# Banded attention and a mixture of adapters: wider q/k transposes, single PSUM banks, half-batch v slots and a planner that counts program fetches

## The chip, the cores and the metric

The kernel runs on one core of a Trainium2 chip. The metric is the device time of one execution in microseconds (us), lower is better. TensorE (PE in the profile) multiplies and transposes, VectorE (DVE), ScalarE (ACT) and GpSimd (POOL) do elementwise work, and SyncE (SP) issues transfers. All of them work from SBUF, the on-chip memory; TensorE writes its results to PSUM, a small memory of eight banks, from where VectorE and ScalarE carry them back to SBUF.

## The reference

q, k and v have 8 batches, 8 heads, 576 positions and 64 values per head, in 32-bit floats. Attention sees only 32 positions to each side. Its result, with the heads side by side, is a table of 4608 rows of 512, and goes through a mixture of 8 low-rank adapters of rank 16, of which each row uses the best two.

```python
scores = scale * np.matmul(q, k.transpose(0, 1, 3, 2))
mask = np.abs(pos[:, None] - pos[None, :]) <= window          # window = 32
attn = softmax(np.where(mask, scores, -1e9))
x = np.matmul(attn, v)  ->  [B * S, H * D] = [4608, 512]

logits = x @ w_gate                                           # [4608, 8]
w = softmax over the best two of the 8 logits
out = x + sum over these two experts e of  w * ((x @ A[e]) @ B[e])
```

## The kernel before

Work is in 16-bit floats. The heads of a batch are handled in pairs (4 pairs a batch, 32 in all), and one head of a pair lies in the upper 64 partitions, the other in the lower.

**Loads.** q and k are cut across batches into 9 tiles of 128 groups of 16 positions. GpSimd issues their loads (`load`), which also turn them to 16 bits. v comes on SyncE in four transfers a batch (`load_v`), and GpSimd casts each half batch with one instruction (`cast_v`) into a table with a column of ones, which later yields the softmax sum.

**Transposes.** `trans` turns a tile of q or k so that head values lie on partitions. It does so with 64x64 pieces: for each of 16 positions, both halves of the rows and both heads, which is 64 matmuls for a tile of q and 64 for one of k, each with its weight load. All go to one PSUM slot of two banks, and `evac` carries the slot out in one instruction, q on VectorE into `qT`, k on ScalarE into `kT`. The first tile is split into two halves.

**Attention.** `score` puts the mask into PSUM by four matmuls and adds 16 score matmuls; `expo` takes the exponential on ScalarE. There are 36 such groups. `pv` multiplies with v in 36 matmuls for a pair, and `norm` divides on VectorE and writes `xs`.

**Adapters.** Once a batch: `moe_xT` transposes x (20 matmuls), `moe_ex` carries that out on VectorE, `moe_zl` computes the low-rank product and the logits, `copy_z` brings these to SBUF, `gate1`, `gate_e` and `gate2` find the best two and their weights, `gate3` multiplies by the weights, `moe_zT` and `moe_ez` transpose, `moe_pd` multiplies with B and adds x, `moe_eo` carries out and `moe_st` stores in three parts. `gate3` runs on GpSimd, except in the last batch, where it runs on VectorE (`DIRECT`).

**Order.** No loop runs on the chip. Every piece of work is a task with an engine, an estimated duration, a due time, what it depends on, and the slots it takes and drops. `Planner.run` plays these tasks through in Python when the kernel is built: whenever an engine is free it starts the ready task with the earliest due time for which slots are left. The resulting order is written out as one straight program for each engine, and each engine then works in that order, waiting on semaphores for its inputs. So GpSimd, SyncE and the others stand before a waiting instruction with everything behind it waiting too. An estimate in the planner never delays anything on the chip by itself; it only moves tasks in that order.

**Slots.** PSUM is one pool `W` of four slots of two banks. v has two slots of a whole batch before the cast (`NVR`) and three after it (`NVB`), and the output five (`NOB`). `GATE` makes the load of k of tile t follow the cast of the first half of v of batch t - 2 in GpSimd's order, for t from 2 to 8; tile 1 has no such rule. `WDEP` names the v load after which the adapter weights are loaded.

Of the kernel before, what the change touches and what calls it, by code (L numbers as in the profile page):

```python
# [23 lines left out]
class Planner:  # L24
# [4 lines left out]
    STICK = 0.3  # L29
    SWITCH = 0.12  # L30

# [7 lines left out]

    def add(self, name, eng, dur, due, emit, deps=(), take=(), drop=(), lat=None, pkt=1.0,  # L40
            cap=1.0, mode=None):
        t = dict(name=name, eng=eng, dur=dur, due=due, emit=emit, deps=list(deps),
                 take=list(take), drop=list(drop), lat=self.LAT if lat is None else lat,
                 n=len(self.tasks), pkt=pkt, cap=cap, mode=mode)
        assert name not in self.by_name, name
        self.tasks.append(t)
        self.by_name[name] = t
        return name

    def run(self):  # L50
# [9 lines left out]
        held = {}  # L60
# [3 lines left out]
        done = []  # L64

# [21 lines left out]
        while events:  # L87
# [17 lines left out]
            while drops and drops[0][0] <= now + 1e-9:  # L105
                _, _, (p, key) = heapq.heappop(drops)
                self.slots[p].append(held.pop((p, key)))
            for e in engines:
# [3 lines left out]
                for t in sorted(ready[e], key=lambda t: (  # L112
                        t["due"] + (self.STICK if t["mode"] != last_mode else 0.0), t["n"])):
                    if all(self.slots[p] for p, _ in t["take"]):
                        break
                else:
                    continue
                ready[e].remove(t)
                for p, key in t["take"]:
                    s = self.slots[p].pop(0)  # L120
                    held[p, key] = s
                t["start"] = now
                end = now + t["dur"] + (self.SWITCH if t["mode"] != last_mode else 0.0)
                mode[e] = t["mode"]
# [21 lines left out]
def kernel(  # L146
# [35 lines left out]
    VQ = (("SP", 0.7, "Q1", nc.sync), ("SP", 0.7, "Q1", nc.sync))  # L182
    GATE = {t: [f"cv{t - 2}.0"] for t in range(2, 9)}
    GATE[1] = []
    WDEP = ["lv1.0.0"]
# [4 lines left out]
    NRAW, NKB, NVR, NVB, NPT, NX, NOB, NW = 3, 3, 2, 3, 6, 4, 5, 4  # L190
# [3 lines left out]
    vraw = [const.tile([128, NP * NB, D], F32, name=f"vraw{i}") for i in range(NVR)]  # L194
    vbd = [const.tile([128, NP * NB, VD], F16, name=f"vbd{i}") for i in range(NVB)]
# [9 lines left out]
    W16 = [w.bitcast(F16) for w in W]  # L205

# [10 lines left out]
    P.pool("W", NW)  # L217
# [8 lines left out]
    P.pool("rc", 3)  # L226
    place = {}

    def slot(p, key):
        return place[p, key]  # L230

# [50 lines left out]
    def vparts(b):  # L282
        return ((0, 18), (18, 36))

    def load_v(b, m0, m1, h):
        hh = (h + m0 // 18) % 2
        src = v[b].rearrange("(hh n) s d -> hh (n s) d", hh=2)[hh].rearrange(
            "(m p) d -> p m d", p=64)
        VQ[h][3].dma_start(out=vraw[slot("vr", b)][64 * h:64 * h + 64, m0:m1], in_=src[:, m0:m1])

# [30 lines left out]
    for b in range(B):  # L321
        for n, (m0, m1) in enumerate(vparts(b)):
            for h in range(2):
                due = 4 * b - 5.8 + 0.5 * n + 0.2 * h - (2 if b == B - 1 else 0)
                P.add(f"lv{b}.{n}.{h}", VQ[h][0], VQ[h][1], due,
                      lambda b=b, m0=m0, m1=m1, h=h: load_v(b, m0, m1, h),
                      prev, take=[] if n or h else [("vr", b)], lat=1.2)
                prev = [f"lv{b}.{n}.{h}"]
                P.add(f"dv{b}.{n}.{h}", VQ[h][2], 2.15 * (m1 - m0) / 36, 0, None, prev, lat=0.8,
                      pkt=14.7, cap=0.82)  # L330
    P.add("ldw", "SP", 2.0, -2, load_w, WDEP, lat=1.2)
    P.add("dw", "Q1", 1.7, -10, None, ["ldw"], lat=0.8, pkt=18.0)
# [3 lines left out]
    def cast_v(b, m0, m1):  # L336
        o = vbd[slot("vb", b)][:, m0:m1, 0:D]
        i_ = vraw[slot("vr", b)][:, m0:m1]
        nc.gpsimd.affine_select(out=o, in_=i_, compare_op=ALU.is_ge, fill=0.0,  # L339
                                base=1, channel_multiplier=0,  # L340
                                pattern=[[0, m1 - m0], [0, D]])

    for b in range(B):
        vp = vparts(b)
        for m, (m0, m1) in enumerate(vp):
            P.add(f"cv{b}.{m}", "POOL", 0.15 + 0.064 * (m1 - m0), 4 * b + 2 * m / len(vp) - 1.5,
                  lambda b=b, m0=m0, m1=m1: cast_v(b, m0, m1),
                  [f"dv{b}.{m}.{h}" for h in range(2)] + ([f"cvb{b}"] if b < NVB else [])
                  + ([f"cv{b}.{m - 1}"] if m else []),
                  take=[] if m else [("vb", b)], drop=[("vr", b)] if m == len(vp) - 1 else [])  # L350


    def trans(t, w, h0, h1):
        src = raw[2 * slot("raw" + "qk"[w], t) + w]
        tp = W16[slot("W", ("t", t, w, h0))].rearrange("p (h r i) -> p h r i", h=2, i=64)
        for r in range(RR):
            for h in range(h0, h1):
                p = slice(64 * h, 64 * h + 64)
                for hh in range(2):
                    nc.tensor.matmul(out=tp[64 * hh:64 * hh + 64, h, r],  # L360
# [3 lines left out]
    def evac(t, w, h0, h1):  # L364
        tp = W16[slot("W", ("t", t, w, h0))].rearrange("p (h r i) -> p h r i", h=2, i=64)[:, h0:h1]
        if w == 0:
            nc.vector.tensor_copy(  # L367
                out=qT[:, :, PADQ + 128 * t + 64 * h0:PADQ + 128 * t + 64 * h1].rearrange(
                    "p r (h i) -> p h r i", i=64),
                in_=tp)  # L370
        else:
            nc.scalar.copy(  # L372
                out=kT[slot("kT", t)][:, 64 * h0:64 * h1].rearrange("p (h i) r -> p h i r", i=64),
                in_=tp.rearrange("p h r i -> p h i r"))

    for t in range(NTI):
        hs = ((0, 1), (1, 2)) if t in SPLIT else ((0, 2),)
        for w in range(2):
            for y, (h0, h1) in enumerate(hs):
# [3 lines left out]
                P.add(f"tr{t}.{w}.{y}", "PE", 1.05 if f == 1 else 0.75,  # L383
# [3 lines left out]
                      take=[("W", ("t", t, w, h0))] + ([("kT", t)] if w and y == 0 else []),  # L387
                      drop=[("raw" + "qk"[w], t)] if last else [])
                P.add(f"e{'qk'[w]}{t}.{y}", "ACT" if w else "DVE",
                      (0.2 + 1.5 * f) if w else (0.12 + 1.1 * f), due,  # L390
                      lambda t=t, w=w, h0=h0, h1=h1: evac(t, w, h0, h1),
                      [f"tr{t}.{w}.{y}"], drop=[("W", ("t", t, w, h0))])
# [6 lines left out]
    def score(t):  # L399
        ps = W[slot("W", ("s", t))].rearrange("p (e i c) -> p e i c", e=2, c=128)  # L400
# [22 lines left out]
    def expo(t):  # L423
        nc.scalar.activation(out=PTs[slot("PT", t)].rearrange("p e i c -> p (e i c)"),  # L424
                             in_=W[slot("W", ("s", t))],
# [12 lines left out]
    for t in range(NT):  # L438
        need = set()
        for g in blocks(t):  # L440
            lo, hi = 4 * g - 2, 4 * g + 5
            for z in (max(lo, 0), min(hi, NI - 1)):
                tt = z // 128
                need.add((tt, (z % 128) // 64 if tt in SPLIT else 0))
# [3 lines left out]
              dep + ["mask", "pad", "ident"], take=[("W", ("s", t)), ("PT", t)], drop=drop)  # L448
# [4 lines left out]
    def pv(u):  # L453
        b, n = divmod(u, NP)
        e, m = divmod(n, 2)
        po = W[slot("W", ("p", u))].rearrange("p (h c) -> p h c", h=2)
        vb = vbd[slot("vb", b)]

        def one(hh, hb, j):
# [8 lines left out]
                rhs=vb[p0:p0 + 64, NB * n + a, :],  # L468
# [9 lines left out]
    def norm(u):  # L478
        b, n = divmod(u, NP)
        po = W[slot("W", ("p", u))].rearrange("p (h c) -> p h c", h=2)[:, :, 0:NG * VD]  # L480
# [13 lines left out]
    for k_, u in enumerate(order):  # L494
# [3 lines left out]
        if k_ % NP == NP - 1:  # L498
            drop.append(("vb", b))
# [4 lines left out]
              take=[("W", ("p", u)), ("rc", u)] + ([("xs", b)] if n == 0 else []), drop=drop)  # L504
# [5 lines left out]
    GX = ((0, 1, 2, 3), (4,))  # L510

    def moe_xT(b, j):
        x = xs[slot("xs", b)]
        tp = W16[slot("W", ("x", b, j))]
        for m, g in enumerate(GX[j]):
# [5 lines left out]
    def moe_ex(b, j):  # L521
        n = len(GX[j])
        nc.vector.tensor_copy(  # L523
            out=xT[b % 2][:, GX[j][0]:GX[j][0] + n].rearrange("p g c k -> p (g c k)"),
            in_=W16[slot("W", ("x", b, j))][:, 0:512 * n])

    def moe_zl(b):
        pz = W[slot("W", ("z", b))]
# [11 lines left out]
    def copy_z(b):  # L540
        pz = W[slot("W", ("z", b))][:, 0:GS * NG].rearrange("p (g c) -> p g c", c=GS)
        nc.scalar.copy(out=zls[b % 2], in_=pz[:, :, 0:ER + E])

    def zlog(b):
        if b in DIRECT:
            pz = W[slot("W", ("z", b))][:, 0:GS * NG].rearrange("p (g c) -> p g c", c=GS)
# [23 lines left out]
    def gate3(b):  # L570
        z = zlog(b)[0]
        lm, m2, s, gate = (gt[x][b % 2] for x in ("lm", "m2", "s", "gate"))
        eng = nc.vector if b in DIRECT else nc.gpsimd
# [3 lines left out]
    def moe_zT(b):  # L577
        zs = zss[b % 2].rearrange("p g e r -> p g (e r)")
        tp = W16[slot("W", ("y", b))]
# [4 lines left out]
    def moe_ez(b):  # L584
        tp = W16[slot("W", ("y", b))][:, 0:128 * NG]
# [3 lines left out]

    def moe_pd(b, j):  # L590
        pd = W[slot("W", ("d", b, j))].rearrange("p (i c) -> p i c", c=DD)
# [8 lines left out]
    def moe_eo(b, j):  # L600
        n = len(GG[j])
        pd = W[slot("W", ("d", b, j))].rearrange("p (i c) -> p i c", c=DD)
        nc.scalar.copy(out=obs[slot("ob", (b, j))][:, 0:n], in_=pd[:, 0:n])  # L603

    def moe_st(b, j):
        ob = obs[slot("ob", (b, j))]
        if len(GG[j]) == 2 and j:
            r0 = S * b + 128 * GG[j][0] - 32
            nc.sync.dma_start(out=out[r0:r0 + 256].rearrange("(i p) c -> p i c", p=128), in_=ob)
            return  # L610
        for i, g in enumerate(GG[j]):
            lo, hi = (32 if g == 0 else 0), (96 if g == NG - 1 else 128)
            r0 = S * b + 128 * g - 32
            nc.sync.dma_start(out=out[r0 + lo:r0 + hi], in_=ob[lo:hi, i])

    for b in range(B):
        d0 = 4 * b + 4.6
        for j in range(2):
            n = len(GX[j])
            P.add(f"xT{b}.{j}", "PE", 0.24 * n, d0 + 0.1 * j, lambda b=b, j=j: moe_xT(b, j),  # L620
                  [f"nm{u}" for u in range(4 * b, 4 * b + 4)]
                  + ([f"zl{b - 2}"] if b >= 2 else []), take=[("W", ("x", b, j))], mode="full")
            P.add(f"exx{b}.{j}", "DVE", 0.1 + 0.28 * n, d0 + 0.1 * j - 0.5, lambda b=b, j=j: moe_ex(b, j),
                  [f"xT{b}.{j}"], drop=[("W", ("x", b, j))])
        P.add(f"zl{b}", "PE", 1.29, d0 + 0.5, lambda b=b: moe_zl(b),
              [f"exx{b}.{j}" for j in range(2)] + ["cw"], take=[("W", ("z", b))], mode="full")
        dr = b in DIRECT
        if not dr:
            P.add(f"cz{b}", "ACT", 0.85, d0 - 1, lambda b=b: copy_z(b), [f"zl{b}"]
# [4 lines left out]
        P.add(f"g2{b}", "DVE", 1.15, d0 - 1, lambda b=b: gate2(b), [f"ge{b}"])  # L634
# [59 lines left out]
```

## Time and profile before

| what | before |
|---|---|
| time, median of 3 runs | 166.75 us (165.22 to 166.88) |
| span of the profiled execution | 167.0 us, mean TensorE clock 0.877 of full |
| all transfers | 29.34 MB, mean 176 GB/s |
| v loads | 32 of 288 KB, median 7.3 us from issue to landing |
| transposes of q and k (L360) | 1152 matmuls, busy 18.6 us |
| carrying them out (L367, L372) | VectorE 1222 ns a tile, ScalarE 1870 ns a tile |
| carrying out x (L523) | VectorE 1220 ns and 412 ns a batch |
| gate product (L574, L575) | GpSimd 253 and 1277 ns; VectorE, in the last batch, 201 and 825 ns |

The profile is one execution. Line numbers (L360) are those of the kernel before. Busy times of TensorE overlap, since its matmuls run in a pipeline, so the sum of a row says little about how long a group holds the engine; the time from one group's start to the next does. Each wait is put down to the event that ended it; "issue" stands where the profile shows no such event. The clock is the share of its full speed that TensorE was granted.

### The profile page before, as it was taken

Reading aid. Unit: us, or ns where it says so; the run is one execution under the profiler, and the core shown is the slowest. Engines: PE = TensorE matmul, PEld = TensorE weight load, DVE = VectorE, ACT = ScalarE, POOL = GpSimd, SP = SyncE. Lnnn points to the kernel's source line nnn. Section 1 sums busy time; section 2 is a strip of 40 time slices with the busy share of each in tenths; the row PEclk is TensorE's granted clock in tenths of the full one; section 3 lists DMA queues with packets and bytes.
Section 4 is the critical chain, followed back from the end, with each engine's and each line's share of the span. In section 5 each row is a group of like instructions: output and inputs, shape, how many; then the busy total and the mean of one; then the engine's idle time right before and its main releaser. Section 6 shows DMA issues by size and latency. Waiting matters only on the chain.

```text
span 167.0 us, 7557 instructions
## 1 busy us (share of the span) xinstructions
PE 104.2 (62%) x3464; PEld 77.2 (46%) x3464; DVE 67.8 (41%) x164; ACT 83.6 (50%) x94; POOL 54.0 (32%) x76
## 2 busy tenths in 40 slices
PE   0259536480975857736478678775667989386350
PEld 0247425470864634326457554544457467274110
DVE  0011520270745625225265834763460958542300
ACT  3214706432044497584036479744669796416160
POOL 7950710745030779800000683900063030210000
PEclk9999955558589999996789999999999999959785
DMA  5999999999979669999996279999630254404434
GB/s 86 215 222 224 189 215 226 212 203 206 214 180 205 116 122 183 215 253 221 342 231 164 50 103 253 296 183 216 225 98 4 92 205 145 142 4 147 138 112 171
DMA packets 49008, 29.34 MB, mean 176 GB/s; under 512 B 39632, under 2 KB 39632, under 8 KB 48976
## 3 DMA queue, kind: packets, MB, share of 16 engines
q1 hardware_dynamic: 43824, 19.42, 44.2%
q0 software_dynamic: 5152, 9.44, 33.3%
q8 instruction: 27, 0.44, 1.1%
q14 instruction: 5, 0.04, 0.1%
HBM read 28.85 MB, written 9.44 MB: 229 GB/s over the span
## 4 chain that ended last, share of the span: by engine, by line
PE 39%; issue 30%; DMA 12%; DVE 6%; ACT 4%; POOL 4%; POOLq 1%; ACTq 1%; SPq 0%; DVEq 0%
PE W L518 6%; PE W L465 5%; PE W L360 5%; DMA vraw<-in_v_dram 5%; PE W L594 5%; DMA raw<-in_q_dram 5%; PE W L416 5%; PE W L596 4%; PE W L531 4%; PE W L404 4%; POOL vbd L339 2%; DMA out_dram<-ob 2%; DVE xs L484 2%; ACT PT L424 2%; DVE qT L367 1%
## 5 line engine op out<-in xcount | busy, mean ns | idle before, releaser
L424 ACT ACTIVATE PT<-W 128x1024 f16<-128x1024 f32 x36 | 35.6, 1031 | 29.1 <-PE W L416 25.0
L360 PE MATMUL W<-ident,raw 64*64 64x64 f16 x1152 | 18.6, 210 | 21.4 <-issue 10.9
L465 PE MATMUL W<-vbd,PT 64*64 64x65 f16 x1152 | 19.0, 205 | 16.0 <-issue 11.5
L339 POOL TENSOR_SCALAR_AFFINE_SELECT vbd<-vraw 128x1152 f16<-128x1152 f32 x16 | 20.3, 1274 | 25.6 <-DMA vraw<-in_v_dram 25.5
L603 ACT COPY ob<-W 128x1024 f32<-128x1024 f32 (+1 forms) x24 | 20.6, 872 | 15.7 <-PE W L596 13.0
L360 PEld LDWEIGHTS <-raw 64*64 64x64 f16 x1152 | 16.3, 123 | 22.9 <-issue 12.8
L484 DVE TENSOR_TENSOR xs<-W,rc 128x640 f16<-128x640 f32 x32 | 26.4, 825 | 1.1
L372 ACT COPY kT<-W 128x2048 f16<-128x2048 f16 (+1 forms) x10 | 17.0, 1698 | 18.7 <-PE W L360 18.7
L465 PEld LDWEIGHTS <-PT 64*64 64x64 f16 x1152 | 15.4, 118 | 21.0 <-issue 17.2
L483 DVE RECIPROCAL rc<-W 128x10 f32<-128x10 f32 x32 | 6.9, 217 | 42.2 <-PE W L465 41.3
L416 PE MATMUL W<-qT,kT 64*64 64x128 f16 x576 | 20.4, 246 | 4.3 <-issue 2.8
L574 POOL TENSOR_TENSOR gate<-lm,s 128x40 f32<-128x40 f32 x7 | 1.8, 253 | 65.0 <-DVE s L568 65.0
L416 PEld LDWEIGHTS <-kT 64*64 64x64 f16 x576 | 17.0, 124 | 10.1 <-issue 7.3
L367 DVE COPY qT<-W 128x2048 f16<-128x2048 f16 (+1 forms) x10 | 11.2, 1116 | 24.0 <-PE W L360 24.0
L518 PE MATMUL W<-ident,xs 128*128 128x128 f16 x160 | 14.2, 253 | 6.5 <-issue 5.5
L404 PE MATMUL W<-mask,ident 64*64 64x512 f16 x144 | 17.9, 458 | 0.0
L523 DVE COPY xT<-W 128x2048 f16<-128x2048 f16 (+1 forms) x16 | 12.5, 816 | 10.9 <-PE W L518 10.9
L594 PE MATMUL W<-Bsb,zT 128*128 128x512 f16 x40 | 16.4, 409 | 0.8 <-ACT zT L586 0.8
L518 PEld LDWEIGHTS <-xs 128*128 128x128 f16 x160 | 12.3, 126 | 8.4 <-issue 6.0
L596 PE MATMUL W<-xs,po__107 128*128 128x512 f16 x40 | 16.0, 401 | 0.0
L531 PE MATMUL W<-WA,xT 128*128 128x136 f16 x160 | 11.4, 226 | 1.7 <-issue 1.2
L531 PEld LDWEIGHTS <-xT 128*128 128x128 f16 x160 | 10.0, 99 | 3.0 <-issue 1.3
(40 smaller groups left out, 82.3 us busy)
## 6 DMA issues: line engine op xcount, KB each, us to landing
vraw<-in_v_dram SPq DMA_DIRECT2D x32, 288.0 KB, 7.3
out_dram<-ob SPq DMA_DIRECT2D x8, 512.0 KB, 9.9
out_dram<-ob SPq DMA_DIRECT2D x16, 192.0 KB, 3.6
out_dram<-ob SPq DMA_DIRECT2D x8, 256.0 KB, 2.9
raw<-in_k_dram POOLq DMA_DIRECT2D x4, 256.0 KB, 6.8
raw<-in_q_dram POOLq DMA_DIRECT2D x4, 256.0 KB, 6.1
raw<-in_k_dram POOLq DMA_DIRECT2D x2, 448.0 KB, 6.5
raw<-in_q_dram POOLq DMA_DIRECT2D x2, 448.0 KB, 7.7
```

Of the source, the lines that this page charges most:

```text
L339: nc.gpsimd.affine_select(out=o, in_=i_, compare_op=ALU.is_ge, fill=0.0, base=1, channel_multiplier=0, pattern=[[0, m1 - m0], [0, D]])
L360: nc.tensor.matmul(out=tp[64 * hh:64 * hh + 64, h, r], lhsT=src[p, hh, D * r:D * r + D], rhs=ident[p, p], is_transpose=True, start=True, s ...
L404: nc.tensor.matmul(out=ps[o0:o0 + 64, e], lhsT=ident[p0:p0 + 64, p0:p0 + 64], rhs=bcast(mask[p0:p0 + 64].rearrange("p h r s -> p (h r s)") ...
L416: nc.tensor.matmul(out=ps[o0:o0 + 64, e, i], lhsT=kT[slot("kT", g // 32)][p0:p0 + 64, c1:c1 + 4].rearrange("p s r -> p (s r)"), rhs=qT[p0: ...
L424: nc.scalar.activation(out=PTs[slot("PT", t)].rearrange("p e i c -> p (e i c)"), in_=W[slot("W", ("s", t))], func=AF.Exp, scale=1.0 / floa ...
L465: nc.tensor.matmul(out=po[o0:o0 + 64, hh, c0:c0 + VD], lhsT=PTs[slot("PT", s // 4)][p0:p0 + 64, e, s % 4, 64 * (1 - j):64 * (1 - j) + 64], ...
L484: nc.vector.tensor_tensor(out=xs[slot("xs", b)].rearrange("p g (h m d) -> p h g m d", h=2, d=D)[:, :, :, n], in0=pog[:, :, :, 0:D], in1=bc ...
L518: nc.tensor.matmul(out=tp[:, o:o + 128], lhsT=x[:, g].rearrange("p (k c) -> p c k", c=4)[:, c], rhs=ident, is_transpose=True, start=True, ...
L531: nc.tensor.matmul(out=pz[:, GS * g:GS * g + ER + E], lhsT=xT[b % 2][:, g, c, :], rhs=WA_sb[:, c, :], start=(c == 0), stop=(c == NP - 1))
L594: nc.tensor.matmul(out=pd[:, i], lhsT=zTs[b % 2][:, g], rhs=B_sb, start=True, stop=False)
L596: nc.tensor.matmul(out=pd[:, i], lhsT=po_, rhs=x[:, g], start=False, stop=True)
L603: nc.scalar.copy(out=obs[slot("ob", (b, j))][:, 0:n], in_=pd[:, 0:n])
```

## The change

The edits, in the order of the code:

- The planner gets an estimate of program fetches: TensorE tasks say how many matmuls they hold (`ni`), and each crossing of 128 matmuls (`LINE`) costs at least 3.6 us since the last (`FETCH`). Due times get an offset for each kind of task (`LEAN`), and several duration estimates are altered.
- PSUM becomes one pool `H` of eight single banks. Work that needs two takes an even bank and the next (`"W"`), the rest takes one.
- Transposes of q and k of all tiles but the first use all 128 rows and 64 columns: 32 matmuls for each instead of 64. Each half of the result has a bank, and is carried out by an instruction of its own.
- x is transposed and carried out in parts of 2, 2 and 1 row groups, instead of 4 and 1.
- v slots hold half a batch: five before the cast and six after it. A pool `ring` of three limits, in the planner alone, how many v transfers are under way. The adapter weights come after all of v of batch 1.
- The load of k of tile 1 is to follow the first cast of v. The rule for the other tiles is the same as before.
- `gate3` runs on VectorE in every batch.
- The output has four slots instead of five.

```diff
+    LEAN = {"cv": 4.05, "cvb": 0.12, "cz": 1.73, "ek": 3.86, "eo": 4.52, "eq": 0.17,
...
+    LINE = 128
+    FETCH = 3.6
+
+    def fetched(self, t, now, end):
+        pos, n = self.pos, t["ni"]
+        self.pos = pos + n
+        k = -(-(pos + 1) // self.LINE) * self.LINE
+        late = 0.0
+        while n and k < pos + n:
+            at = now + late + (end - now) * (k - pos) / n
+            late += max(0.0, self.line - at)
+            self.line = max(at, self.line) + self.FETCH
+            k += self.LINE
+        return end + late
...
+                if e == "PE":
+                    end = self.fetched(t, now, end)
...
-    GATE = {t: [f"cv{t - 2}.0"] for t in range(2, 9)}
-    GATE[1] = []
-    WDEP = ["lv1.0.0"]
+    GATE = {t: [f"cv{t - 2}.0"] for t in range(2, NTI)}
+    GATE[1] = ["cv0.0"]
+    WDEP = ["lv1.1.1"]
...
-    NRAW, NKB, NVR, NVB, NPT, NX, NOB, NW = 3, 3, 2, 3, 6, 4, 5, 4
+    NRAW, NKB, NVR, NVB, NPT, NX, NOB, NW = 3, 3, 5, 6, 6, 4, 4, 4
+    HV = NP * NB // 2
...
-    vraw = [const.tile([128, NP * NB, D], F32, name=f"vraw{i}") for i in range(NVR)]
-    vbd = [const.tile([128, NP * NB, VD], F16, name=f"vbd{i}") for i in range(NVB)]
+    vraw = [const.tile([128, HV, D], F32, name=f"vraw{i}") for i in range(NVR)]
+    vbd = [const.tile([128, HV, VD], F16, name=f"vbd{i}") for i in range(NVB)]
...
-    P.pool("W", NW)
+    P.pool("H", 2 * NW)
...
+    def trans_full(t, w):
+        src = raw[2 * slot("raw" + "qk"[w], t) + w]
+        for r in range(RR):
+            tp = H16[slot("H", ("t", t, w, r // 8))]
+            for hh in range(2):
+                nc.tensor.matmul(out=tp[64 * hh:64 * hh + 64, 128 * (r % 8):128 * (r % 8) + 128],
+                                 lhsT=src[:, hh, D * r:D * r + D], rhs=ident,
+                                 is_transpose=True, start=True, stop=True)
...
+    def evac(t, w, h):
+        if t not in SPLIT:
+            tp = H16[slot("H", ("t", t, w, h))].rearrange("p (r i) -> p r i", i=128)
+            if w == 0:
+                c0 = PADQ + 128 * t
+                nc.vector.tensor_copy(out=qT[:, 8 * h:8 * h + 8, c0:c0 + 128], in_=tp)
+            else:
+                nc.scalar.copy(out=kT[slot("kT", t)][:, :, 8 * h:8 * h + 8],
+                               in_=tp.rearrange("p r i -> p i r"))
+            return
...
-    GX = ((0, 1, 2, 3), (4,))
+    PB = {1: "H", 2: "W"}
...
-        eng = nc.vector if b in DIRECT else nc.gpsimd
+        eng = nc.vector
```

## The prediction

> **What bounds the kernel now.** I read the queues and waits of the page first, then the waits of TensorE alone, its timeline, the table by stage, and last GpSimd's timeline.
>
> The page, parts 1 and 3 (busy time; DMA queue: packets, MB, share):
>
> ```profile
> PE 104.2 (62%) x3464; PEld 77.2 (46%) x3464; DVE 67.8 (41%) x164; ACT 83.6 (50%) x94; POOL 54.0 (32%) x76
> ...
> q8 instruction: 27, 0.44, 1.1%
> ```
>
> No engine is full. The second line is the clue: 27 packets carry instructions. 3464 matmuls and as many weight loads are 6928 instructions; 6928 / 27 = 257 to a packet, so one packet brings 128 matmuls with their weight loads. I call that a line of the program; there are 3464 / 128 = 27.1.
>
> The waits of TensorE (who waited <- releaser: us, times, longest):
>
> ```profile
> PE W L465 <- issue: 11.5, 7, 4.0
> PE W L360 <- issue: 10.9, 6, 2.6
> PE W L360 <- DMA raw<-in_k_dram: 6.8, 2, 5.8
> PE W L518 <- issue: 5.5, 3, 3.4
> PE W L581 <- DVE zs L575: 3.1, 1, 3.1
> ...
> PE W L416 <- issue: 2.8, 3, 1.2
> ...
> PE W L581 <- POOL zs L575: 2.3, 1, 2.3
> ...
> PE W L531 <- issue: 1.2, 1, 1.2
> ```
>
> "issue" is waiting that no semaphore explains: 11.5 + 10.9 + 5.5 + 2.8 + 1.2 = 31.9 us in 20 pieces, 1.6 us each. The DMA waits are nearly all the first one, before anything has landed. The timeline of TensorE shows what the pieces are:
>
> ```profile
> 37.27 0.44 PE L465 MATMUL W<-vbd,PT 64*64 64x65 f16 x25
> 41.69 0.38 PE L465 MATMUL W<-vbd,PT 64*64 64x65 f16 x11 [3.98 <-issue]
> ```
>
> TensorE stops in the middle of one group of 36 matmuls that needs nothing new. Counting matmuls along that timeline, the restarts at 62.69, 69.16, 75.36, 81.55, 86.38, 90.38, 95.20 and 98.93 us are exactly 128 matmuls apart, whatever stands there. So TensorE waits for its own program. Restart to restart takes 3.5 to 7.8 us, of which 0.5 to 4.0 us is the stop.
>
> The table by stage says why the trip is long (columns: window, width, busy us of each engine, granted clock, DMA share, GB/s):
>
> ```profile
> 20.00:48.00 28.00, 15.42 (x537) 12.68 (x538) 10.51 (x18) 9.35 (x9) 9.42 (x13) 0.57 1.06 202
> 48.00:92.00 44.00, 29.64 (x1080) 22.23 (x1080) 18.75 (x43) 24.02 (x28) 14.27 (x19) 0.92 0.94 208
> 92.00:120.00 28.00, 19.05 (x728) 13.86 (x729) 15.01 (x36) 18.08 (x21) 11.74 (x14) 1.00 0.84 181
> 120.00:145.00 25.00, 20.52 (x742) 14.76 (x737) 14.76 (x42) 18.28 (x22) 5.50 (x6) 1.00 0.39 131
> ```
>
> To 92 us the DMA engines are full with q, k and v[...]; from 116 us on, with few loads left, restarts are 3.5 to 5.1 us apart. From 20 to 145 us the bound is TensorE's program supply, on DMA engines that are nearly a bound themselves.
>
> GpSimd's timeline:
>
> ```profile
> 69.10 1.18 POOL L279 DMA_DIRECT2D raw<-in_q_dram  x2
> 93.18 0.25 POOL L574 TENSOR_TENSOR gate<-lm,s 128x40 f32<-128x40 f32 x1 [22.91 <-DVE s L568]
> 93.51 1.27 POOL L575 TENSOR_TENSOR zs<-zl,gate 128x640 f16<-128x640 f32 x1
> ```
>
> Its queue stands 22.9 us before a gate product, with the load issues of the next tile behind it.
>
> [...]
>
> **The change, part by part.**
>
> Transposes. For 8 of 9 tiles, q and k, 64 matmuls become 32: 8 x 2 x 32 = 512 fewer. 3464 - 512 = 2952, or 23.1 lines instead of 27.1: 4 trips less. Each new matmul moves 128 columns over all rows, on two halves of the columns. Nearest row: the score matmuls move 128 columns on four quarters, 16 of them in 0.24 us (at 90.96 us in the chain of waits), so 60 ns for the four at once; on two halves that is 30 ns each and 32 x 30 = 1.0 us. Ends: 0.85 us by the column rate alone (the 128x512 matmuls take 0.22 us, so 53 ns for 128 columns), and 2.0 us if the halves do not overlap. The 64 old ones take about 0.63 us (in the same chain 0.54 for 63 at 58.81 us, 0.70 for 64 at 65.97 us). I take 1.0: 16 x 0.37 = 6 us more TensorE work[...].
>
> What that does to stalls. From 20 to 145 us: 125 us less 32 of stall and about 5 of other waits leaves 88 us of work. The table has 537 + 1080 + 728 + 742 = 3087 matmuls there, 24.1 lines, so 3.7 us a line. After: 7 of the 8 tiles lie in the window, so 88 + 5 = 93 us and 3087 - 448 = 2639 matmuls, 20.6 lines, 4.5 us a line. Restart to restart periods in before were (us) 6.4, 4.5, 7.8, 6.5, 4.5, 6.5, 6.2, 6.2, 4.8, 4.0, 4.8, 3.7, 5.9, 4.8, 6.7, 3.5, 5.1, 3.7. Taken as trips, what is over 4.5 sums to about 17 us. So stall falls from 32 to about 17, work rises by 5: TensorE gains 10 us. Most of the extra transposing is free because it fills time that was stall.
>
> Gate product to VectorE. GpSimd loses 1.8 + 8.9 us; VectorE gains 7 x (0.20 + 0.825) = 7.2 us (its rows for the last batch). The engine handover goes, and GpSimd's queue no longer stops for it. On TensorE's path: the 2.3 us wait at L581, at 146 us, mostly goes. I count 2. The 3.1 us of the last batch stays; it was on VectorE already. Loads go out earlier, but TensorE hardly waits for raw after 20 us, so that by itself is worth nothing.
>
> Evacuations by halves. q on VectorE: 16 x 0.69 instead of 8 x 1.22, +1.3 us. xT: 2 x 0.69 instead of 1.22 a batch, +1.3 us. k on ScalarE: 16 x 1.01 instead of 15.0, +1.2 us. VectorE comes to 78 us, ScalarE to 85, in over 140: hidden beside TensorE. Halves come free sooner, but TensorE shows few waits for PSUM (2.3 for PT, 0.9 for xs), so single banks gain at most 1 us; counted 0.
>
> v by half batches. The same 32 loads of 288 KB. SyncE waited only 2.6 us for a v slot, TensorE 0.3 us for a cast. Counted 0, as are the smaller output ring (4 for 5; three stores a batch against a batch every 11 us or more) and the deeper memsets.
>
> The added wait: tile 1's k load now follows the first cast of v on GpSimd. It went out at 7.18, the cast was at 10.16, so k goes 4 us later and the q behind it 1.2 us later; TensorE's transposes of tile 1 (18.09 us) wait for them. Against that, v has less traffic beside it. Between -1.5 and +1.2 us; counted 0.
>
> Planner. Charging 3.6 us a line and shifted due times alter the order on every engine. No row prices this. Nothing lost if TensorE stays full, up to 8 us gained if stalls fall on idle spots; I count 3.
>
> Sum: 166.75 - 10 - 2 - 3 = 151.75, put at 151.
>
> **Rivals.** (a) The supply sets all of it: a line costs its trip whatever is in it. Then 4 lines x 4.9 us = 20 us and the 2 of the gate go: 145. For it: the exact 128 spacing. Against: 4.5 us of work a line nears the trip. (b) The DMA engines take the gain: loads come closer together, trips lengthen, each boundary still stalls 1.6 us. Then 4 x 1.6 = 6.4 saved, 5 spent on transposes, 2 for the gate: 163. For it: DMA at 0.94 to 92 us, and loads that cannot end much before 115. Against: 47 us remain after the last load, in which DMA is at a third. (c) Slower: the two halves do not overlap and each group takes 2.0 us. 16 x 1.4 = 22 us more, of which stalls hide 15, and the new order loses 0 to 4: 171 to 177, say 172. [...] Against: quarters overlap well today.
>
> **How the numbers follow.** The forecast 0.54, (a) 0.22, (b) 0.14, (c) 0.10. The forecast spreads from 147 to 157 with the planner's 0 to 8. The range 142 to 164 takes in the forecast, three quarters of (a) and half of (b): 0.54 + 0.16 + 0.07 = 0.77, near 8 in 10. Faster by over 1%: all but (c) and the slow end of (b), 0.87. Within 1%: 0.04. Slower: 0.09.
>
> **What would show it.** Right: 23 instruction packets; "issue" waits of TensorE at 13 to 21 us; a transpose group of 32 in 0.85 to 1.1 us; no gate product on GpSimd, and no idle stretch of 20 us between its load issues; the last 20 us, from the last transposes of x to the store, as before. Wrong: issue waits still near 32 us (b), under 10 with the same work (a), transposes at 2 us (c), or a new wait of TensorE for q, k or v of over 5 us after 20 us.

## The result, and the profile after

| | before | after |
|---|---|---|
| time, median | 165.99 us (163.64 to 166.88, 4 runs) | 156.05 us (155.06 to 157.51, 4 runs) |
| ratio, 95% interval | | 0.947 (0.931 to 0.963) |
| span of the profiled execution | 167.0 us | 153.4 us |

Faster by 5%, inside the range of 142 to 164, but 5 us short of the 151 that was forecast. Times of runs are medians, and each ratio comes from runs on the same chip as those of the kernel before, whose median was 165.8 to 168.4 us on the chips used. The ratios compare only the faster executions of each kernel, so they differ by up to 2% from the ratio of the medians beside them. Executions of one kernel scatter by 1 to 7% from the fastest to the slowest, so differences of a per cent between chips mean nothing.

The page after, parts 1 and 3:

```profile
PE 108.3 (71%) x2952; PEld 80.6 (53%) x2952; DVE 80.1 (52%) x197; ACT 84.1 (55%) x102; POOL 43.4 (28%) x62
...
q8 instruction: 23, 0.38, 1.0%
```

2952 matmuls in 23 packets: four trips fewer. The waits of TensorE after:

```profile
PE W L546 <- issue: 6.7, 6, 2.0
...
PE W L419 <- issue: 4.8, 2, 2.4
PE W L662 <- DVE zs L656: 3.2, 1, 3.2
PE W L419 <- DMA raw<-in_q_dram: 2.6, 1, 2.6
...
PE W L497 <- issue: 2.0, 3, 0.9
...
PE W L599 <- issue: 0.6, 1, 0.6
```

Waits without a releaser sum to 14.1 us, from 31.9; the forecast was about 17. The price is in the timeline of TensorE:

```profile
57.27 1.08 PE L419 MATMUL W<-ident,raw 128*64 128x128 f16 x32
58.29 0.39 PE L680 MATMUL W<-Bsb,zT 128*128 128x512 f16 x1
```

From the start of a group of 32 wide transposes to the start of what follows it is 1.02 us (forecast 1.0). The stages after:

```profile
20.00:48.00 28.00, 19.90 (x595) 16.31 (x591) 12.65 (x25) 12.98 (x14) 9.64 (x12) 0.94 1.12 214
48.00:92.00 44.00, 34.92 (x979) 26.43 (x982) 29.41 (x72) 28.56 (x37) 14.41 (x18) 0.96 0.97 207
92.00:120.00 28.00, 24.15 (x728) 17.35 (x716) 19.41 (x48) 20.25 (x26) 6.47 (x6) 1.00 0.85 205
```

Between 20 and 48 us TensorE is busy for 19.9 us where it was 15.4, and its waits without a releaser fall there from 10.8 to 4.4 us. The clocks printed for this stage, 0.94 and 0.57, cannot be set against each other: 32 wide transposes at 24.03 us took 1.92 us, nearly twice the 1.08 us of those at 28.85 us, although the clock printed for both is 1.00. GpSimd's timeline after has no gate product, but its queue does not run free:

```profile
84.16 1.19 POOL L346 DMA_DIRECT2D raw<-in_q_dram  x2
97.38 1.27 POOL L401 TENSOR_SCALAR_AFFINE_SELECT vbd<-vraw 128x1152 f16<-128x1152 f32 x1 [12.03 <-DMA vraw<-in_v_dram]
```

The idle stretch before the gate product is gone; one of 12 us, before a cast of v, stands between the load issues. TensorE's last wait for q or k ends at 24.03 us and it has none for a cast of v, so the 12 us do not reach it.

### The profile page after: what moved, and what is told of

The parts are those of the page before. It is cut to its first block, busy times and chain, and to the rows that moved or that the text cites. A ratio compares the mean times of both kernels' runs of the same rounds, so it can differ in the third digit from the quotient of the medians.

```text
span 153.4 us, 6568 instructions
## 1 busy us (share of the span) xinstructions
PE 108.3 (71%) x2952; PEld 80.6 (53%) x2952; DVE 80.1 (52%) x197; ACT 84.1 (55%) x102; POOL 43.4 (28%) x62
## 3 DMA queue, kind: packets, MB, share of 16 engines
HBM read 28.85 MB, written 9.44 MB: 250 GB/s over the span
## 5 line engine op out<-in xcount | busy, mean ns | idle before, releaser
L505 ACT ACTIVATE PT<-W 128x1024 f16<-128x1024 f32 x36 | 35.2, 1036 | 16.0 <-PE W L497 15.4
L565 DVE TENSOR_TENSOR xs<-W,rc 128x640 f16<-128x640 f32 x32 | 26.4, 824 | 1.1
L419 PE MATMUL W<-ident,raw 128*64 128x128 f16 x512 | 19.0, 232 | 8.9 <-issue 4.8
L546 PE MATMUL W<-vbd,PT 64*64 64x65 f16 x1152 | 17.5, 199 | 8.9 <-issue 6.7
L419 PEld LDWEIGHTS <-raw 128*64 128x64 f16 x512 | 16.6, 117 | 11.2 <-issue 10.4
L546 PEld LDWEIGHTS <-PT 64*64 64x64 f16 x1152 | 13.8, 111 | 14.5 <-issue 11.3
L444 ACT COPY kT<-W 128x1024 f16<-128x1024 f16 x16 | 15.7, 1021 | 9.3 <-PE W L419 9.2
L604 DVE COPY xT<-W 128x1024 f16<-128x1024 f16 (+1 forms) x24 | 13.6, 594 | 10.3 <-PE W L599 8.8
L442 DVE COPY qT<-W 128x1024 f16<-128x1024 f16 x16 | 10.6, 686 | 12.7 <-PE W L419 11.9
L564 DVE RECIPROCAL rc<-W 128x10 f32<-128x10 f32 x32 | 6.9, 215 | 15.3 <-PE W L546 13.8
L599 PE MATMUL W<-ident,xs 128*128 128x128 f16 x160 | 12.3, 229 | 1.5 <-DVE xT L604 0.8
L599 PEld LDWEIGHTS <-xs 128*128 128x128 f16 x160 | 10.4, 118 | 2.8 <-issue 1.7
L433 PE MATMUL W<-ident,raw 64*64 64x64 f16 x128 | 4.3, 239 | 9.2 <-POOL mask L318 6.0
```

Of the source, the lines that this page charges most:

```text
L419: nc.tensor.matmul(out=tp[64 * hh:64 * hh + 64, 128 * (r % 8):128 * (r % 8) + 128], lhsT=src[:, hh, D * r:D * r + D], rhs=ident, is_transp ...
L546: nc.tensor.matmul(out=po[o0:o0 + 64, hh, c0:c0 + VD], lhsT=PTs[slot("PT", s // 4)][p0:p0 + 64, e, s % 4, 64 * (1 - j):64 * (1 - j) + 64], ...
L565: nc.vector.tensor_tensor(out=xs[slot("xs", b)].rearrange("p g (h m d) -> p h g m d", h=2, d=D)[:, :, :, n], in0=pog[:, :, :, 0:D], in1=bc ...
L599: nc.tensor.matmul(out=tp[:, o:o + 128], lhsT=x[:, g].rearrange("p (k c) -> p c k", c=4)[:, c], rhs=ident, is_transpose=True, start=True, ...
```

## Experiments

**The changed kernel again, on a second chip.**

> The changed kernel once more, on the chip of these comparisons: 155 to 158 us, 0.93 to 0.96 of the kernel before.

156.64 us against 168.35, ratio 0.920 (0.912 to 0.928), a little below the expected 0.93 to 0.96. Issue waits are 16.1 us. So the change is worth 5 to 8%, depending on the chip's runs.

**Wide transposes alone, in the old order.**

```diff
 def trans(t, w, h0, h1):
...
+    if t not in SPLIT:
+        tw = W16[slot("W", ("t", t, w, h0))].rearrange("p (r i) -> p r i", i=128)
+        for r in range(RR):
+            for hh in range(2):
+                nc.tensor.matmul(out=tw[64 * hh:64 * hh + 64, r],
+                                 lhsT=src[:, hh, D * r:D * r + D], rhs=ident,
+                                 is_transpose=True, start=True, stop=True)
+        return
```

(`evac` reads the new layout, still with one instruction a tile; not shown.)

> The kernel before, in its own order and with its own slots; only the transposes of 8 tiles are 128x64, 32 matmuls for 64. Program supply theory: 23 instruction packets, TensorE's issue waits fall from 32 us to about 17, a transpose group rises from 0.63 to 1.0 us, time near 156 us (153 to 160). Order theory (the gain comes from the planner's new order): issue waits may fall, but other waits take their place, and the time stays at 163 to 167 us. DMA theory (the transfers are the bound): the same, 163 us or more.

160.4 us against 168.35 on the same chip as the run above, ratio 0.935 (0.929 to 0.942): 10 to 12 us by the ratio and 8 by the medians, from this one edit. The waits of TensorE:

```profile
PE W L480 <- issue: 7.6, 4, 3.1
...
PE W L533 <- issue: 3.0, 2, 2.5
PE W L546 <- issue: 2.8, 2, 2.4
PE W L596 <- POOL zs L590: 2.3, 1, 2.3
```

7.6 + 3.0 + 2.8 = 13.4 us of issue waits, 18.5 less than before. The order and the DMA theories fall for this part: nothing else of the change was in this kernel, the other waits of TensorE stayed near what they were (24.6 us before, 26.4 here), and the time moved. A higher clock may have had a part: the mean granted clock was 0.930 in this profile and 0.877 in the one before. But 9 of the 16 groups of wide transposes took 1.8 to 1.9 us here, against 1.08 us for the rest, and the kernel gained all the same.

**The changed kernel with the old transposes.**

```diff
 def trans(t, w, h0, h1):
-    if t not in SPLIT:
-        return trans_full(t, w)
```

(`evac` takes its layout for split tiles for all of them; the plan is untouched, so the order is still the one planned for 32 matmuls a group.)

> The changed kernel with its order, slots and banks; only the transposes are 64x64 again, 64 matmuls for 32. Supply theory: 27 packets, issue waits back to 25 to 32 us, against 6 us less transposing: 160 to 165 us. Order theory: 152 to 157 us, since TensorE has less work and the order is kept.

173.48 us, ratio 1.023 (1.016 to 1.030): slower than the kernel before, and 0.102 above the changed kernel on the same chip, 17 us. That is more than the supply theory gave. Its waits:

```profile
PE W L431 <- issue: 21.7, 8, 4.5
...
PE W L544 <- issue: 5.1, 4, 2.1
...
PE W L495 <- issue: 1.2, 2, 1.1
```

28.7 us of issue waits in all, of which 0.7 at a line not shown, and 21.7 inside the transposes themselves (L431), in 8 stops of up to 4.5 us. 64 small matmuls for q and 64 for k are 128, a whole line, and at the 0.63 us that 64 took in the kernel before they are done in about 1.3 us (an estimate). In this order the same edit is worth half as much again as in the old one, or more; the order was planned for the wide transposes.

**The gate product back on GpSimd.**

```diff
-        eng = nc.vector
+        eng = nc.vector if b in DIRECT else nc.gpsimd
```

> The changed kernel with the gate product of batches 0 to 6 back on GpSimd, at the same place of the planner's order. Supply theory, which counted 2 us for this edit: 157 to 159 us. Rival (GpSimd's queue was what held loads back): GpSimd stands before gate products with q and k loads behind, TensorE waits for raw, 162 us or more.

157.89 us, ratio 0.918 (0.912 to 0.925), against 0.920 for the changed kernel: no difference. The wait that this part of the change was to take away is there in both, with another engine's name:

```profile
PE W L662 <- POOL zs L656: 3.2, 1, 3.2
...
PE W L419 <- DMA raw<-in_q_dram: 2.6, 1, 2.6
```

The changed kernel has the same 3.2 us with "DVE zs", and the same 2.6 us for q. In this order GpSimd's queue did not hold the loads back, and the end of the program waits for the chain of gate steps, on whichever engine its last step runs.

**Without the due-time offsets and the charge for fetches; then without each of them alone.**

```diff
-    LEAN = {"cv": 4.05, "cvb": 0.12, "cz": 1.73, "ek": 3.86, "eo": 4.52, "eq": 0.17,
...
+    LEAN = {}
...
-    FETCH = 3.6
+    FETCH = 0.0
```

(The altered duration estimates and the pool `ring` stay.)

> The changed kernel without due-time offsets (LEAN empty) and without the charge for fetches (FETCH 0), so all edits but the planner's. Wide transposes alone gave 0.935 of before, the whole change 0.920. If the planner's part is what lies between: 0.93 to 0.94. If the planner's order matters more with these slots: over 0.95. If it is a loss by its tail: under 0.92.

167.55 us against 165.75, ratio 1.018 (1.010 to 1.027), so the branch "over 0.95" holds: the order matters more with these slots. This kernel has the wide transposes, and the fewest issue waits so far (11.3 us), and it is still no faster than before. Its waits:

```profile
PE W L658 <- DVE zs L652: 6.4, 3, 2.8
PE W L493 <- issue: 3.4, 1, 3.4
PE W L595 <- DVE xs L561: 3.1, 3, 2.5
PE W L595 <- issue: 2.5, 2, 1.9
PE W L595 <- DVE qT L438: 2.0, 1, 2.0
```

Summed over all lines, TensorE waits 23.4 us for VectorE and ScalarE here, 13.8 in the changed kernel and 9.8 in the kernel with wide transposes alone. Their growth is about as large as the gain of the transposes.

> The changed kernel with due-time offsets and FETCH 0: the planner no longer counts the program's lines. If counting lines lets it put dense groups apart: 1 to 4 us slower than the changed kernel (0.925 to 0.945), with issue waits above 16 us. If it is only bookkeeping: 0.915 to 0.925.

158.13 us against 165.75, with 14.4 us of issue waits where the changed kernel has 14.1 and 16.1. That is outside both expected bands for the ratio, but the changed kernel was not run on this chip, and against its 156.05 and 156.64 us elsewhere a difference of 2 us cannot be told from that of the chips. The stalls did not grow, so counting lines in the planner looks like bookkeeping.

> The changed kernel with FETCH 3.6 and LEAN empty. Together with the run that has neither it says which of the two orders the work better. If the offsets carry the gain: 0.93 or more. If the offsets cost (they put the adapters of the last two batches side by side): 0.90 to 0.915, with 20 to 22 us from the last product with v to the end.

169.41 us against 165.75, in executions from 162.9 to 172.4 us. The waits for VectorE and ScalarE are 23.8 us. So it is the offsets that make the other edits pay: 158 us with them and no charge for fetches, 168 to 169 us without them, with the charge or without it.

**Transposes and offsets, without the rest.**

```diff
+    LEAN = {"cv": 4.05, "cvb": 0.12, "cz": 1.73, "ek": 3.86, "eo": 4.52, "eq": 0.17,
...
-        t = dict(name=name, eng=eng, dur=dur, due=due, emit=emit, deps=list(deps),
+        t = dict(name=name, eng=eng, dur=dur, due=due + self.LEAN.get(kind, 0.0), emit=emit, deps=list(deps),
```

(on top of the kernel with wide transposes alone)

> The kernel before with 128x64 transposes and the table of due-time offsets, and with nothing else of the change: two-bank slots, whole-batch v slots, x carried out in two parts, the gate product on GpSimd, no charge for fetches. If the transposes and the offsets are the whole gain: 0.92 to 0.94. If the offsets only fit the new slots and banks: 0.95 or more. If the other edits are a loss that the offsets only repair: under 0.92.

157.85 us against 167.32, ratio 0.947 (0.935 to 0.959). The interval takes in both of the first two branches. On the old slots and engines the offsets add nothing that can be told from the 0.935 of the transposes alone. They are worth something only beside the other edits: single banks, three parts of x, half-batch slots and the gate on VectorE, taken together, lose the gain without them, and with them give it back and 1 to 2% more, 0.920 against 0.935 on one chip.

**The last batch but one sooner.**

```diff
-        d0 = 4 * b + 4.6
+        d0 = 4 * b + 4.6 - (2 if b == B - 2 else 0)
```

The changed kernel ends with the adapters of two batches side by side. Its timeline:

```profile
128.30 0.48 PE L546 MATMUL W<-vbd,PT 64*64 64x65 f16 x36
...
138.10 0.71 PE L662 MATMUL W<-ident,zs 128*128 128x128 f16 x5 [3.24 <-DVE zs L656]
139.59 0.69 PE L662 MATMUL W<-ident,zs 128*128 128x128 f16 x5 [0.78 <-ACT zT L667]
```

The last product with v is over at 128.8 us and the span ends at 153.4: 24.6 us. Before, the last products with v were these:

```profile
143.76 0.64 PE L465 MATMUL W<-vbd,PT 64*64 64x65 f16 x52 [1.04 <-ACT PT L424]
```

They ended at 144.4 and the span at 167.0: 22.6 us.

> The changed kernel, with all adapter tasks of the last batch but one due 2 us earlier, so that its transposes of x and its low-rank product come ahead of the last batch's last product with v, and its gates run beside that. Tail theory (two batches' adapters end side by side, and 2 to 4 us of the forecast went there): the last product with v ends 1 to 2 us later than in the changed kernel, the end comes 19 to 21 us after it and not 24.6; 152 to 155 us on a chip where the changed kernel takes 156, ratio 0.90 to 0.915. Rival (the last batch's own chain sets the end whatever runs beside it): 156 us, 0.92.

156.87 us against 165.75, ratio 0.940 (0.931 to 0.949): not faster than the changed kernel elsewhere (0.920), nor clearly than the kernel without the charge for fetches on this chip (158.13 us, with 24.7 us after its last product with v). The shortened end is there, as its timeline shows, but the last product with v comes later by more than that:

```profile
134.99 0.81 PE L546 MATMUL W<-vbd,PT 64*64 64x65 f16 x72
138.07 1.31 PE L599 MATMUL W<-ident,xs 128*128 128x128 f16 x20 [2.27 <-DVE xs L565]
140.91 0.71 PE L662 MATMUL W<-ident,zs 128*128 128x128 f16 x5 [1.53 <-DVE zs L656]
```

It ends at 135.8, and the span at 157.5, 21.7 us after. Some of the 7 us may be this execution's, which took 159.16 us; but the work that was moved ahead of it also took its place in the queue, and the next transposes wait 2.27 us for its result. The tail theory is right on the order and wrong on the gain.

**The added wait taken out.**

```diff
     plan = P.run()
+    at = {t["name"]: i for i, t in enumerate(plan)}
+    plan.insert(at["cv0.0"], plan.pop(at["ld1.1.0"]))
```

> The changed kernel with one task moved: on GpSimd the load of k of tile 1 is issued ahead of the first cast of v, as before the change; everything else keeps its order. Counted 0 (between -1.5 and +1.2 us): 0.92 to 0.945, within 1% of the changed kernel, and TensorE's wait for q of tile 1, 2.6 to 4 us, shrinks by no more than 2. If the added wait costs time: 2 us or more faster.

159.64 us against 167.32, ratio 0.962 (0.950 to 0.974), above the expected 0.92 to 0.945: not faster than the changed kernel, so no cost of the wait shows. GpSimd's timeline says why; here it is without the wait:

```profile
7.15 1.18 POOL L346 DMA_DIRECT2D raw<-in_k_dram  x2
10.77 1.28 POOL L401 TENSOR_SCALAR_AFFINE_SELECT vbd<-vraw 128x1152 f16<-128x1152 f32 x1 [2.44 <-DMA vraw<-in_v_dram]
17.27 1.27 POOL L401 TENSOR_SCALAR_AFFINE_SELECT vbd<-vraw 128x1152 f16<-128x1152 f32 x1 [5.21 <-DMA vraw<-in_v_dram]
18.48 1.18 POOL L346 DMA_DIRECT2D raw<-in_q_dram  x2
```

and in the changed kernel:

```profile
8.70 1.28 POOL L401 TENSOR_SCALAR_AFFINE_SELECT vbd<-vraw 128x1152 f16<-128x1152 f32 x1 [1.50 <-DMA vraw<-in_v_dram]
9.94 1.19 POOL L346 DMA_DIRECT2D raw<-in_k_dram  x2
14.15 1.27 POOL L401 TENSOR_SCALAR_AFFINE_SELECT vbd<-vraw 128x1152 f16<-128x1152 f32 x1 [3.02 <-DMA vraw<-in_v_dram]
15.37 1.19 POOL L346 DMA_DIRECT2D raw<-in_q_dram  x2
```

Issued first, k goes 2.8 us sooner, but v lands 2 to 3 us later beside it, and the q behind the casts goes 3.1 us later; TensorE waits 6.0 us for that q instead of 2.6. The changed kernel took 156.64 us on this chip in an earlier comparison, 3 us less, so the added wait may be a gain; the two were not run side by side. This profile also has 21.0 us of issue waits, with the same instructions on TensorE as the changed kernel with its 14.1 and 16.1: the number of packets alone does not fix the stalls.

**Half of v not loaded, in both kernels.**

```diff
-        nc.sync.dma_start(out=vraw[slot("vr", (b, e))][64 * h:64 * h + 64],
-                          in_=src[:, HV * e:HV * e + HV])
+        nc.sync.dma_start(out=vraw[slot("vr", (b, e))][64 * h:64 * h + 64, 0:HV // 2],
+                          in_=src[:, HV * e:HV * e + HV // 2])
```

(and the same in the kernel before; the places left out are zeroed once at the start)

> The kernel before with the same half of v not loaded. Supply theory: issue waits fall from 32 us to 18 to 24, time 154 to 159 us, and the restarts come 3.6 to 5 us apart in the first 90 us too. Neither: issue waits stay at 28 us or more and the time above 163.

163.73 us against 167.32, ratio 0.989 (0.977 to 1.000). The stages and the waits of TensorE:

```profile
20.00:48.00 28.00, 17.41 (x683) 14.83 (x685) 11.48 (x22) 11.40 (x12) 8.50 (x10) 0.70 0.85 164
48.00:92.00 44.00, 31.95 (x1157) 23.63 (x1145) 21.38 (x51) 25.56 (x29) 18.43 (x24) 0.84 0.66 144
```

```profile
PE W L364 <- issue: 11.9, 5, 4.2
PE W L469 <- issue: 7.5, 6, 2.3
...
PE W L522 <- issue: 5.2, 2, 3.9
```

The DMA engines are at 0.66 from 48 to 92 us where they were at 0.94, and 11.9 + 7.5 + 5.2 = 24.6 us of issue waits are still there, single ones of 4.2 us too. The stalls lie just above the supply theory's 18 to 24 us and below the 28 of its opposite, and the time is on the side of the opposite. A sixth less traffic over the whole span, a third less from 48 to 92 us, came with a quarter less stall and 1 to 2% less time.

> The changed kernel with half of v not loaded (the second half of each transfer's rows is left out, and its place is zeroed once at the start), so about 22 us less work for the DMA engines with the same program. Supply theory, trips lengthened by the transfers: issue waits fall from 14-16 us to 6-10, time to 146 to 151 us. DMA theory (the transfers are what holds the changed kernel): 140 us or less. Neither (trips have their length whatever is queued): issue waits stay at 13 us or more.

152.41 us against 167.32, ratio 0.911 (0.890 to 0.933), with 13.2 us of issue waits. The DMA theory, 140 us or less, falls: with about 22 us less to move (an estimate: half of the 32 loads of 288 KB, at the 205 to 214 GB/s of the stages above) the changed kernel stays above 150, some 4 us below its 156.64 on this chip earlier. The supply theory's 6 to 10 us of stalls falls as well.

## Why the prediction was right, and where it was off

**Transposes and stalls: right.** The steps were 512 matmuls less, 23 packets, a group at 1.0 us, stalls from 32 to about 17 and a gain of 10 us on TensorE. Measured: 2952 matmuls, 23 packets, 1.02 us, 14.1 and 16.1 us, and 8 to 12 us for that edit alone in the old order. The estimate of 30 ns for a wide transpose, from the score matmuls, fits at a granted clock of 1.00: the dense group of 32 at 57.27 us took 1.02 us, 32 ns each. The prediction had no term for groups that take nearly twice as long. In the profile of that edit alone, whose span is 5.9 us shorter than before, the stalls fell by 18.5 us instead of 15 and the work grew by about 11 us instead of 5 to 6, in part because 9 of 16 groups took 1.8 to 1.9 us. The two errors partly cancel, so that the net came so near to 10 is in part luck. Rival (c), halves that do not overlap, is out, and so is (a): four whole trips would have been 20 us.

**Gate product, counted 2: failed.** The step read the 2.3 us wait on GpSimd as the price of the engine. It is the gate chain's: in the new order it is 3.2 us on either engine.

**Planner, counted 3: failed as a separate term.** "Nothing lost if TensorE stays full" did not hold: without the offsets the other edits lose everything the transposes won (1.018). With them, all the edits beside the transposes together come to a ratio of 0.920 against 0.935, about 2.5 us (3.8 by the medians), on one chip. In the first comparison the whole change gained 9.9 us, no more than the transposes do alone. So the 5 us for gate and planner became 0 to 4, which is part or all of the distance from 151 to 156.

**Edits counted 0: half right.** VectorE at 78 us was put down as hidden beside TensorE. It is at 80.1 us, but in what order its work comes decides: 23.4 us of waits on VectorE and ScalarE without offsets, 13.8 with them. A share of busy time could not show that. Which of these edits brings the waits was not separated, so single banks, parts of x and half-batch slots have no price of their own here.

**Last 20 us "as before": wrong.** From the last product with v to the end it is 24.6 us instead of 22.6, as two batches end together. Moving one of them ahead cut it to 21.7 us and won nothing, since the last product with v came later by more.

**Why the trips are long: not borne out.** The prediction blamed full DMA engines, and rival (b) rested on that. With half of v gone, three quarters of the stalls remain, and the trips are no shorter where the traffic fell most (last section). With one profile of each kernel, a small share of the traffic in the stalls is not ruled out. What was right needed only the trips' measured length, not their cause.

## What to carry to other kernels

When an engine stops in the middle of a group that needs nothing, count its instructions between restarts. Here the same count of 128 each time pointed to its program, and fewer, larger instructions paid (a ratio of 0.935 for that edit alone) although a group took 1.02 us instead of about 0.63. An order tuned to one set of slots and durations belongs to that set: here the same offsets were worth nothing on the old slots and the whole gain on the new ones. A wait need not be worth its length, as the one for the gate product was not: ask what its end depends on before crediting its removal.

## What the runs showed of the hardware

TensorE's stops with no releaser ("issue") ended at a near-fixed distance from an instruction packet: 2.2 to 3.0 us after its start in the kernel before (20 stops), 2.2 to 2.8 us in the changed kernel (12 stops). The 14 traces of this case have 156 of these stops; each ended 2.2 to 4.0 us after the start of a packet, and all but one within 3.4 us. That ties the stops to the program more closely than the count of 128 does.

The other part of a trip, from the end of a stop to the start of the next packet, varied: 1.5 to 4.8 us in the kernel before (mean 3.1 us, 16 stops before 112 us), 1.1 to 4.2 us with half of v left out (mean 2.6 us, 11 stops). From 48 to 92 us, where the busy share of the DMA engines fell from 0.94 to 0.66, the mean is 2.8 us in both kernels (8 and 5 stops). What sets this part is open; no run shows that it follows the traffic.

Slower work followed some stops. In the kernel without offsets and without the charge TensorE stood for 3.4 us; its timeline:

```profile
77.93 0.42 PE L493 MATMUL W<-qT,kT 64*64 64x128 f16 x7 [3.40 <-issue]
78.29 3.63 PE L415 MATMUL W<-ident,raw 128*64 128x128 f16 x64
...
89.58 1.98 PE L415 MATMUL W<-ident,raw 128*64 128x128 f16 x64
```

The 64 transposes after the stop took 3.63 us, at a granted clock of 0.50; 64 others in the same kernel took 1.98 us, a factor of 1.83. What lowered the clock was not shown. A shorter stop was followed by the same clock in the changed kernel: one of 2.40 us ended at 76.03 us, and the granted clock was 0.50 from 76.54 to 79.95 us.
